# The log sum of the fourth opening block as two passes of an exact pair

## The chip, the cores and the metric

The kernel runs on one core of one Trainium2 chip. The core has five engines that work side by side and wait for each other by semaphores: TensorE (matrix products, PE in the profile; PEld is its loading of the stationary operand), VectorE (DVE), ScalarE (ACT), GpSimd (POOL) and SyncE (SP), which here issues the transfers. The metric is the device time of one execution in microseconds. Before the change the median of three runs is 516.35 us (516.2 to 517.95).

## The reference

A gated linear attention feeds a feed-forward layer with a squared ReLU. All of it is float32.

```python
# q, k, v, alpha: (4, 8, 768, 48); alpha between 0.8 and 1.0
for t in range(S):
    state = alpha[:, :, t, :, None] * state + einsum('bhd,bhe->bhde', k[:, :, t], v[:, :, t])
    y[:, :, t] = einsum('bhd,bhde->bhe', q[:, :, t], state)
x = y.transpose(0, 2, 1, 3).reshape(3072, 384)
h = maximum(x @ w_in, 0.0)            # w_in: (384, 2048)
return (h * h) @ w_out                # w_out: (2048, 384)
```

## The kernel before

The recurrence is done in chunks of 128 steps. A block is one chunk of one of the four sequences, with all eight heads side by side (128 x 384 values of each of q, k, v and alpha), so there are 24 blocks; block n is chunk n // 4 of sequence n % 4. Four blocks make a group of 512 tokens, and the feed-forward layer is done by groups, six in all. A block's attention goes in small steps, named by short words:

- `ln`: the logarithm of alpha, on ScalarE, in place.
- `cs`: the running sum of the logarithms over the 128 steps, a product with a triangle of ones on TensorE. In blocks from `AT['split']` on, a step `sp` ahead of it splits the logarithm into a pair: `hi`, the value rounded to TensorE's fast float32 type (fp32r), and `lo`, what is left of it, in the same type. The sum is then two fast passes, one over each part, into the same bank. In blocks below `AT['split']`, `cs` is one product in plain float32, which TensorE does as two passes at a lower rate.
- `eb`, `ei`: the exponential of that sum and of its negative, on ScalarE (tiles `b` and `inv`).
- `mq`, `mk`: q times `b` and k times `inv`, on VectorE.
- `qT`, `kT`: both turned round by TensorE; `qc`, `kc` copy the results (`qs`, `ks`) to where TensorE can read them.
- `sc`, `kv`, `am`, `us`, `st`, `lt`: the scores within a chunk, the sums for the state, the mask, and the state of the next chunk.
- `ya`, `yb`: the products that give y for two blocks; `ep` copies y into the feed-forward layer's input `x`, on ScalarE and VectorE.
- `ha`, `hb`: the first layer of the feed-forward for half a group.
- `load`, `weights`: transfers; `first`, `second`: the weights' conversion to float32, on ScalarE and VectorE.

The order of the work is the program's: each engine takes its instructions in the order in which the program writes them, and there is no scheduler that changes it. For the first blocks (the opening, about the first 35 us) that order is the string `AT['first']` in line 22, which is read word by word (line 1004): the word `ln3` calls `ln(3)`, the step of the fourth block. Everything behind the opening is woven from lists of due times (`weave`, line 1113). Transfers all go through SyncE's queue in `move` (line 108), which also holds one back until an earlier one has landed.

Lines that matter for the change: 261 (`ln`), 273 and 274 (`sp`: hi, lo), 283 (`cs` in one product), 286 and 287 (`cs` in two passes), 294 and 298 (`eb`, `ei`), 302 (`mq`, `mk`), 354 (`qT`, `kT`), 368 (the copies `qs`, `ks`), 393 (y), 621 (the copies x<-y), 942 (first layer in the first group). The blocks' tiles `b` and `hi` take turns in one pool of two buffers, and `inv` and `lo` in another.

Of the kernel before, what the change touches and what calls it, by code (L numbers as in the profile page):

```python
# [18 lines left out]


GB = 4
AT = {'sq': (12, 6, 5, 11), 'hi': (12, 13, 11, 10), 'ips': 0, 'evs2': 0.3, 'tc': 'AAAD', 'rest': 0, 'lg': 9, 'lag': 1, 'post2': 1, 'ty': 9, 'thrp': 3.5, 'cvo': 2.9, 'thr': 2.25, 'm48': 16, 'cvs': 3.6, 'cv1': 0.25, 'later': (0, 2, 0, 4, 1, 4, 2), 'evs': 0.35, 'lead': 4, 'post': 3, 'w_first': (48.95, 42.05, 53.75), 'wstep': 0.8, 'w_in_at': 1.25, 'w_in_by': 2.9, 'room1': 23, 'room': 24, 's0': 4, 'ahead': 6, 'late': 2, 'xs': 0.55, 'g0': ((3.25, 4, False, True, 32.0), (22.75, 6, True, True), (26.5, 8, True, False)), 'sc0': (2.95, 2.35, 2.35), 'g1': ((2.75, 8, False, 16.25), (15.5, 10, True), (31.75, 12, True)), 'g': ((2.075, 6, True), (13.75, 8, True)), 'g1x': 49.0, 'gx': 46.25, 'g0x': 55.25, 'k0': 3, 'h0': 12, 'k1': 5, 'h1': 6, 'h1by': 2, 'evs0': 0.3, 'tp': 'ADAD', 'tp1': 'AADA', 'split': 4, 'o0': (34, 46, 46), 'o1': (), 'o2': (16.75, 19.25, 30.75, 23.0, 38.0), 'str1': 10.0, 'ga': 9.5, 'gb': 12.25, 'cv0': -1.125, 'pre': '1a 0a 0q 0k 1k 1q', 'cp': ('q2a', 'k2b', 'k0a', 'k3a', 'k3b', 'k0b', 'q0b', 'q3b', 'q2b', 'q3a'), 'evd': ((0, 0, 0), (0, 0, 1), (0, 1, 2), (0, 1, 3), (2, 0, 3), (2, 1, 1), (2, 1, 2)), 'first': 'ln0 load1v cs0 ei0 eb0 zeros4 mk0 mq0 qT0 kT0 ln1 cs1 kc0 ei1 warm0 load0v eb1 mk1 qc0 weights0 lt1 sc0 load2a mq1 load2q kT1 kc1 qT1 load2k load3a qc1 load3k kv0 am0 first0 load3v sc1 ln2 kv1 load3q us0 am1 weights6 us1 cs2 ya0 ei2 second0 eb2 lt0 ln3 yb0 load2v mq2 qT2 mk2 load4a ep00 ep01 qc2 kT2 cs3 kc2 eb3 ei3 zeros1 sc2 ep02 mq3 mk3 kT3 ep03 weights2 first1 st0 ha0 second1 lt2 kv2 am2 qT3 load4k kc3 qc3 ha1 weights5 first2 sc3 kv3 am3 load4q us2 ha2 us3 ya2 yb2 weights3 ep20 ep21 ep22 load4v ep23 second2 first3 weights1 st1 weights4 ha3 lt3 hb0 st2 second3 hb2 hb3 hb1 st3'}


RUN = {0: 128, 32: 32, 64: 64, 96: 32}
# [3 lines left out]
def kernel(  # L29
# [78 lines left out]
    def move(us, out, in_):  # L108
        ins = nc.sync.dma_start(out=out, in_=in_).ins  # L109
        ahead = 0.0  # L110
        for before, took in reversed(under_way):
            if ahead >= AT["thrp" if us == 1.0 else "thr"]:
                tc.add_manual_dep(
# [16 lines left out]
    def load(n, xs="aqkv"):  # L130
        c, b = divmod(n, B)
        for x in xs:
            t = tile_of(x, n)
            if id(t) in owner:
                need(("free", *owner[id(t)]))
            owner[id(t)] = x, n
            given.add((x, n))
            move(
                1.1,
                out=t[:, :, 0:D] if x in "qk" else t.rearrange("a (h d) -> a h d", h=H),  # L140
                in_=srcs[x][b, :, c * C : (c + 1) * C, :].rearrange("h s d -> s h d"),
            )
# [57 lines left out]

    for word in AT["pre"].split():
        load(int(word[0]), word[1:])
# [52 lines left out]
    def work(name, bufs=1):  # L255
        return p2.tile([128, NP, C], FP32, tag=name, name=name, bufs=bufs)
# [7 lines left out]

    SPLIT = AT["split"]

    def sp(n):
# [4 lines left out]
        lo = p2.tile([128, H * D], FP32R, tag="inv", name="lo")  # L272
        (nc.scalar.copy if n in AT["hi"] else nc.vector.tensor_copy)(out=hi, in_=la)
        nc.vector.tensor_tensor(out=lo, in0=la, in1=hi.bitcast(FP32), op=ALU.subtract)
# [90 lines left out]
    def copied(x, n):  # L365
        t = blk[n][f"{x}s"] = work(f"{x}s", 2 if x == "k" else 4)
        copy = nc.vector.tensor_copy if f"{x}{n}" in AT["cp"] else nc.scalar.copy
        copy(out=t, in_=blk[n].pop(f"{x}T"))
# [64 lines left out]
    def state_sums(n):  # L433
        need(("v", n), ("kb", n))
        given.add(("free", "k", n))
        ps = two[n]
        m = D if n >= AT["m48"] else 64
        for p in range(NP):
# [805 lines left out]
```

## Time and profile before

| what | value |
| --- | --- |
| median of the runs | 516.35 us |
| lowest, highest of three runs | 516.2, 517.95 us |
| the profiled execution's own time | 516.38 us |
| its span, from the first to the last instruction | 514.6 us |
| TensorE busy | 504.5 us (98%) |
| VectorE busy | 357.7 us (70%) |
| ScalarE busy | 315.5 us (61%) |
| granted clock of TensorE, mean | 1.000 |

All times in the tables of a profile are microseconds from the start of the span. A line of a timeline gives the start, the length, the engine, the line of the kernel, the operation, what it writes and reads, its shape, and how often it stands there in a row; in brackets stands how long the engine had been idle before it and what it was waiting for. Consecutive instructions of one engine can overlap by a little, since they are pipelined. SPq, DVEq and the like are an engine's queue rather than its arithmetic. "issue" is time in which nothing that the profile shows was waited for.

### The profile page before, as it was taken

What the parts mean: (1) busy time and instruction counts of PE and PEld (TensorE: products, weight loads), DVE (VectorE), ACT (ScalarE), POOL (GpSimd) and SP (SyncE); (2) the same over time, 40 slices, a digit from 0 to 9 for tenths busy, and PEclk for the clock granted to TensorE, in tenths of its full rate; (3) what the DMA queues carried; (4) which work ended last, traced back from release to release, by engine and by line L of the source; (5) the groups of instructions that cost most, each with busy time, mean ns of one, the idle gap of its engine ahead of it and who ended that gap; (6) DMA issues with size and microseconds to landing.
All of it is one profiled execution on the core that took longest, in us unless ns stands there. A gap on an engine that the chain in (4) does not pass through costs nothing.

```text
span 514.6 us, 13039 instructions
## 1 busy us (share of the span) xinstructions
PE 504.5 (98%) x5354; PEld 421.1 (82%) x5354; DVE 357.7 (70%) x640; ACT 315.5 (61%) x657; POOL 5.3 (1%) x29
## 2 busy tenths in 40 slices
PE   7799999999999999999999999999999999999997
PEld 5675456689888689888899987799988899988996
DVE  3769799989887498585697377596465396263861
ACT  4789896466988674368672186783175782165620
POOL 4000000000000000000000000000000000000000
PEclk9999999999999999999999999999999999999999
DMA  9899867484869649986984787684673554798101
GB/s 182 201 264 236 271 180 190 107 235 187 274 195 256 164 101 272 333 228 183 227 233 134 262 235 200 173 247 131 231 253 125 182 143 142 251 373 292 61 1 62
DMA packets 139612, 103.12 MB, mean 200 GB/s; under 512 B 109841, under 2 KB 116001, under 8 KB 139553
## 3 DMA queue, kind: packets, MB, share of 16 engines
q1 hardware_dynamic: 139552, 102.30, 69.0%
q8 instruction: 42, 0.69, 0.5%
q14 instruction: 18, 0.14, 0.1%
HBM read 84.95 MB, written 17.33 MB: 199 GB/s over the span
## 4 chain that ended last, share of the span: by engine, by line
PE 94%; DMA 4%; SPq 1%; ACT 0%; DVE 0%; issue 0%; DVEq 0%; POOLq 0%
PE o L825 41%; PE h L731 33%; PE h L942 8%; PE y L393 4%; PE sckv L413 2%; PE T L581 2%; DMA k_in<-in_k_dram 2%; PE sckv L442 2%; DMA qk_lent<-in_q_dram 1%; DMA v_in<-in_v_dram 1%; PE cs L286 1%; PE cs L287 1%; SPq L109 1%; ACT x L621 0%; DVE x L621 0%
## 5 line engine op out<-in xcount | busy, mean ns | idle before, releaser
L731 PE MATMUL h<-xa,wb 128*128 128x512 f32 x240 | 68.9, 395 | 0.0
L731 PE MATMUL h<-xl,wl 128*128 128x512 f32 x240 | 67.7, 390 | 0.0
L731 PE MATMUL h<-xd,wd 128*128 128x512 f32 x240 | 67.2, 395 | 0.0
L748 ACT ACTIVATE h<-h 128x512 f32<-128x512 f32 x44 | 25.6, 581 | 59.0 <-PE h L731 59.0
L825 PE MATMUL o<-wb,ha 128*128 128x384 f32 x176 | 60.0, 341 | 0.0
L825 PE MATMUL o<-wl,hl 128*128 128x384 f32 x176 | 58.9, 335 | 0.0
L621 ACT COPY x<-y 48x256 f32<-48x256 f32 (+3 forms) x133 | 46.6, 366 | 18.7 <-PE y L393 15.8
L825 PE MATMUL o<-wd,hd 128*128 128x384 f32 x320 | 56.4, 334 | 0.0
L825 PEld LDWEIGHTS o<-wd,hd 128*128 128x128 f32 x320 | 55.6, 188 | 0.0
L653 DVE TENSOR_TENSOR hid<-h,hid 128x512 f32<-128x512 f32 x36 | 24.8, 689 | 43.4 <-PE h L731 43.2
L731 PEld LDWEIGHTS h<-xl,wl 128*128 128x128 f32 x240 | 45.1, 188 | 9.8
L731 PEld LDWEIGHTS h<-xa,wb 128*128 128x128 f32 x240 | 44.2, 188 | 9.8 <-ACT qs L591 0.8
L731 PEld LDWEIGHTS h<-xd,wd 128*128 128x128 f32 x240 | 44.2, 188 | 9.4
L825 PE MATMUL o<-wb,hx 128*128 128x384 f32 x144 | 48.2, 335 | 0.0
L825 PE MATMUL o<-wl,hx 128*128 128x384 f32 x144 | 48.1, 334 | 0.0
L942 PE MATMUL h<-x,w_in 128*128 128x512 f32 (+1 forms) x120 | 43.3, 512 | 0.2 <-DVE x L621 0.2
L825 PE MATMUL o<-w_out,hid 128*128 128x384 f32 x128 | 43.1, 490 | 0.0
L706 ACT ACTIVATE ha<-hid 128x512 fp32r<-128x512 f32 x44 | 27.0, 636 | 17.2 <-DVE hl L658 7.4
L825 PEld LDWEIGHTS o<-w_out,hid 128*128 128x128 f32 x128 | 23.9, 190 | 15.6 <-issue 0.5
L746 ACT ACTIVATE hid<-h 128x512 f32<-128x512 f32 x36 | 21.5, 597 | 24.3 <-PE h L731 24.3
L942 PEld LDWEIGHTS h<-x,w_in 128*128 128x128 f32 x120 | 22.1, 190 | 17.3 <-issue 14.8
L658 DVE SCALAR_TENSOR_TENSOR hl<-ha,hid 128x512 fp32r<-128x512 f32 x44 | 30.2, 686 | 6.1 <-ACT ha L706 6.1
(113 smaller groups left out, 867.1 us busy)
## 6 DMA issues: line engine op xcount, KB each, us to landing
wd<-do SPq DMA_DIRECT2D x37, 384.0 KB, 3.6
wl<-lo SPq DMA_DIRECT2D x35, 384.0 KB, 4.3
wl<-li SPq DMA_DIRECT2D x32, 384.0 KB, 2.9
wd<-di SPq DMA_DIRECT2D x32, 384.0 KB, 3.8
raw<-in_moe_w_out_dram SPq DMA_DIRECT2D x8, 767.5 KB
raw<-in_moe_w_in_dram SPq DMA_DIRECT2D x8, 767.2 KB
v_in<-in_v_dram SPq DMA_DIRECT2D x24, 192.0 KB, 3.7
out_dram<-osb SPq DMA_DIRECT2D x24, 192.0 KB, 1.8
```

What stands on the lines that cost most here:

```text
L393: ins = nc.tensor.matmul(out=ys[e][64 * half : 64 * half + D + G * e, m % 2, p // 2, t], lhsT=lhsT, rhs=rhs, start=(half, e) not in seen, ...
L413: nc.tensor.matmul(out=ps[e][HALF[h], 0, p, :], lhsT=ks[rows, p, HALF[h]], rhs=qs[rows, p, HALF[h]], start=True, stop=True, skip_group_che ...
L442: nc.tensor.matmul(out=ps[h][64 * e : 64 * e + m, 1, p, G:64], lhsT=tile_of("k", n)[HALF[h], 2 * p + e, 0:m], rhs=tiles["v"][n % NV][HALF[ ...
L621: copy(out=x[kk][to : to + m, t : t + 2], in_=blk[n]["y"][e][r : r + m, :, p // 2],)
L653: nc.vector.tensor_tensor(out=o, in0=x, in1=z, op=op)
L658: nc.vector.scalar_tensor_tensor(out=o, in0=x, scalar=c, in1=y, op0=ALU.mult, op1=op)
L706: nc.scalar.activation(out=a, in_=x, func=AF.Copy, scale=NEAR * E)
L731: nc.tensor.matmul(out=acc["h", j], lhsT=here[w, "i", p][:, kk, jj * 128 : (jj + 1) * 128], rhs=x_parts[x][:, kk], start=start and kk == 0 ...
L746: nc.scalar.activation(out=hid[j], in_=x, func=AF.Copy, scale=E)
L748: nc.scalar.activation(out=x, in_=x, func=AF.Copy, scale=1.0 + E)
L825: nc.tensor.matmul(out=acc[t][:, 0:DM], lhsT=lhs[:, t * C : (t + 1) * C], rhs=rhs, start=start, stop=stop, skip_group_check=True,)
L942: nc.tensor.matmul(out=ps, lhsT=w[:, kk, c0 : c0 + 128], rhs=xT[g][kk][:, cols], start=(kk == 0), stop=(kk == KM - 1),)
```

## The change

Block 3, the fourth and last block of the first group, gets its logarithm split too. `AT['split']` goes from 4 to 3, so that `sp(3)` and the two passes of `cs(3)` take the place of the one product, and the word `sp3` is put into the opening's order directly behind `ln3`, ahead of `yb0` and of the third block's `mq2` and `mk2`. Block 3 isn't listed in `AT['hi']`, so both instructions of the step go to VectorE.

```diff
 AT = {
...
-'split': 4,
+'split': 3,
...
-'first': '... us1 cs2 ya0 ei2 second0 eb2 lt0 ln3 yb0 load2v mq2 qT2 mk2 load4a ep00 ep01 qc2 kT2 cs3 kc2 eb3 ei3 zeros1 sc2 ep02 mq3 mk3 kT3 ep03 weights2 ...'
+'first': '... us1 cs2 ya0 ei2 second0 eb2 lt0 ln3 sp3 yb0 load2v mq2 qT2 mk2 load4a ep00 ep01 qc2 kT2 cs3 kc2 eb3 ei3 zeros1 sc2 ep02 mq3 mk3 kT3 ep03 weights2 ...'
...
 }
```

The step and the two forms of the sum are there already, for the later blocks:

```python
def sp(n):
    if n < SPLIT:
        return
    la = blk[n].pop("la")
    hi = p2.tile([128, H * D], FP32R, tag="b", name="hi")
    lo = p2.tile([128, H * D], FP32R, tag="inv", name="lo")
    (nc.scalar.copy if n in AT["hi"] else nc.vector.tensor_copy)(out=hi, in_=la)
    nc.vector.tensor_tensor(out=lo, in0=la, in1=hi.bitcast(FP32), op=ALU.subtract)
    blk[n]["parts"] = hi, lo

def cs(n):
    given.add(("free", "a", n))
    ps = blk[n]["cs"] = bank(n, "cs")
    out = ps.rearrange("a p t -> a (p t)")[:, 0 : H * D]
    if n < SPLIT:
        nc.tensor.matmul(out=out, lhsT=causal_r.bitcast(FP32), rhs=blk[n].pop("la"), start=True, stop=True)
        return
    hi, lo = blk[n].pop("parts")
    nc.tensor.matmul(out=out, lhsT=causal_r, rhs=hi, start=True, stop=False)
    nc.tensor.matmul(out=out, lhsT=causal_r, rhs=lo, start=False, stop=True)
```

More of the change, by code (lines that the diff above doesn't have):

```diff
@@ L21 @@
 GB = 4
-AT = {'sq': (12, 6, 5, 11), 'hi': (12, 13, 11, 10), 'ips': 0, 'evs2': 0.3, 'tc': 'AAAD', 'rest': 0, 'lg': 9, 'lag': 1, 'post2': 1, 'ty': 9, 'thrp': 3.5, 'cvo': 2.9, 'thr': 2.25, 'm48': 16, 'cvs': 3.6, 'cv1': 0.25, 'later': (0, 2, 0, 4, 1, 4, 2), 'evs': 0.35, 'lead': 4, 'post': 3, 'w_first': (48.95, 42.05, 53.75), 'wstep': 0.8, 'w_in_at': 1.25, 'w_in_by': 2.9, 'room1': 23, 'room': 24, 's0': 4, 'ahead': 6, 'late': 2, 'xs': 0.55, 'g0': ((3.25, 4, False, True, 32.0), (22.75, 6, True, True), (26.5, 8, True, False)), 'sc0': (2.95, 2.35, 2.35), 'g1': ((2.75, 8, False, 16.25), (15.5, 10, True), (31.75, 12, True)), 'g': ((2.075, 6, True), (13.75, 8, True)), 'g1x': 49.0, 'gx': 46.25, 'g0x': 55.25, 'k0': 3, 'h0': 12, 'k1': 5, 'h1': 6, 'h1by': 2, 'evs0': 0.3, 'tp': 'ADAD', 'tp1': 'AADA', 'split': 4, 'o0': (34, 46, 46), 'o1': (), 'o2': (16.75, 19.25, 30.75, 23.0, 38.0), 'str1': 10.0, 'ga': 9.5, 'gb': 12.25, 'cv0': -1.125, 'pre': '1a 0a 0q 0k 1k 1q', 'cp': ('q2a', 'k2b', 'k0a', 'k3a', 'k3b', 'k0b', 'q0b', 'q3b', 'q2b', 'q3a'), 'evd': ((0, 0, 0), (0, 0, 1), (0, 1, 2), (0, 1, 3), (2, 0, 3), (2, 1, 1), (2, 1, 2)), 'first': 'ln0 load1v cs0 ei0 eb0 zeros4 mk0 mq0 qT0 kT0 ln1 cs1 kc0 ei1 warm0 load0v eb1 mk1 qc0 weights0 lt1 sc0 load2a mq1 load2q kT1 kc1 qT1 load2k load3a qc1 load3k kv0 am0 first0 load3v sc1 ln2 kv1 load3q us0 am1 weights6 us1 cs2 ya0 ei2 second0 eb2 lt0 ln3 yb0 load2v mq2 qT2 mk2 load4a ep00 ep01 qc2 kT2 cs3 kc2 eb3 ei3 zeros1 sc2 ep02 mq3 mk3 kT3 ep03 weights2 first1 st0 ha0 second1 lt2 kv2 am2 qT3 load4k kc3 qc3 ha1 weights5 first2 sc3 kv3 am3 load4q us2 ha2 us3 ya2 yb2 weights3 ep20 ep21 ep22 load4v ep23 second2 first3 weights1 st1 weights4 ha3 lt3 hb0 st2 second3 hb2 hb3 hb1 st3'}
@@ new lines @@
+AT = {'sq': (12, 6, 5, 11), 'hi': (12, 13, 11, 10), 'ips': 0, 'evs2': 0.3, 'tc': 'AAAD', 'rest': 0, 'lg': 9, 'lag': 1, 'post2': 1, 'ty': 9, 'thrp': 3.5, 'cvo': 2.9, 'thr': 2.25, 'm48': 16, 'cvs': 3.6, 'cv1': 0.25, 'later': (0, 2, 0, 4, 1, 4, 2), 'evs': 0.35, 'lead': 4, 'post': 3, 'w_first': (48.95, 42.05, 53.75), 'wstep': 0.8, 'w_in_at': 1.25, 'w_in_by': 2.9, 'room1': 23, 'room': 24, 's0': 4, 'ahead': 6, 'late': 2, 'xs': 0.55, 'g0': ((3.25, 4, False, True, 32.0), (22.75, 6, True, True), (26.5, 8, True, False)), 'sc0': (2.95, 2.35, 2.35), 'g1': ((2.75, 8, False, 16.25), (15.5, 10, True), (31.75, 12, True)), 'g': ((2.075, 6, True), (13.75, 8, True)), 'g1x': 49.0, 'gx': 46.25, 'g0x': 55.25, 'k0': 3, 'h0': 12, 'k1': 5, 'h1': 6, 'h1by': 2, 'evs0': 0.3, 'tp': 'ADAD', 'tp1': 'AADA', 'split': 3, 'o0': (34, 46, 46), 'o1': (), 'o2': (16.75, 19.25, 30.75, 23.0, 38.0), 'str1': 10.0, 'ga': 9.5, 'gb': 12.25, 'cv0': -1.125, 'pre': '1a 0a 0q 0k 1k 1q', 'cp': ('q2a', 'k2b', 'k0a', 'k3a', 'k3b', 'k0b', 'q0b', 'q3b', 'q2b', 'q3a'), 'evd': ((0, 0, 0), (0, 0, 1), (0, 1, 2), (0, 1, 3), (2, 0, 3), (2, 1, 1), (2, 1, 2)), 'first': 'ln0 load1v cs0 ei0 eb0 zeros4 mk0 mq0 qT0 kT0 ln1 cs1 kc0 ei1 warm0 load0v eb1 mk1 qc0 weights0 lt1 sc0 load2a mq1 load2q kT1 kc1 qT1 load2k load3a qc1 load3k kv0 am0 first0 load3v sc1 ln2 kv1 load3q us0 am1 weights6 us1 cs2 ya0 ei2 second0 eb2 lt0 ln3 sp3 yb0 load2v mq2 qT2 mk2 load4a ep00 ep01 qc2 kT2 cs3 kc2 eb3 ei3 zeros1 sc2 ep02 mq3 mk3 kT3 ep03 weights2 first1 st0 ha0 second1 lt2 kv2 am2 qT3 load4k kc3 qc3 ha1 weights5 first2 sc3 kv3 am3 load4q us2 ha2 us3 ya2 yb2 weights3 ep20 ep21 ep22 load4v ep23 second2 first3 weights1 st1 weights4 ha3 lt3 hb0 st2 second3 hb2 hb3 hb1 st3'}
```

## The prediction, made before the result was known

> **What bounds the kernel now.** I read the page first, then the busy time by stretches, the chain of waits in order of time, and last the timelines of VectorE, ScalarE and TensorE around the place of the change. The page:
>
> ```profile
> span 514.6 us, 13039 instructions
> PE 504.5 (98%) x5354; PEld 421.1 (82%) x5354; DVE 357.7 (70%) x640; ACT 315.5 (61%) x657; POOL 5.3 (1%) x29
> ```
>
> TensorE (PE) is busy for all but 10.1 us of the span, so the question is only where those idle microseconds lie. The stretches say it (columns: PE, PEld, DVE, ACT, POOL busy with their counts, granted clock, DMA share, GB/s):
>
> ```profile
> 20.00:30.00 10.00, 8.58 (x177) 6.97 (x177) 7.79 (x17) 8.61 (x20) 0.00 (x0) 1.00 0.89 240
> 30.00:40.00 10.00, 9.66 (x147) 7.57 (x144) 6.76 (x16) 8.84 (x20) 0.00 (x0) 1.00 0.88 264
> 40.00:50.00 10.00, 10.00 (x29) 5.18 (x28) 9.52 (x20) 9.05 (x18) 0.00 (x0) 1.00 1.03 223
> ```
>
> From 40 us on PE has no idle time (50 to 300 us: 250.00 busy of 250; 300 to 400: 99.72) until the last 5 us. Whatever makes PE late before 40 us is therefore carried to the end; nothing behind it can take it up. Before 40 us PE waits, and the chain of waits tells for what (start, length, what):
>
> ```profile
> 17.33 5.48 DMA qk_lent<-in_q_dram
> ...
> 22.90 0.06 DVE qk_lent L302
> ...
> 23.38 0.56 DVE qk_lent L302
> ...
> 24.08 0.63 PE kT L354 x4
> ...
> 33.50 0.36 ACT x L621
> ...
> 36.76 12.31 PE h L942 x38
> ```
>
> The fourth block's q arrives at 22.81; VectorE scales q (step mq3, 22.90) and k (mk3, 23.38); PE turns k (kT3) at 24.08 and is dense from there, but for the hand-over of the second pair's result at 33.5 to 36.8, which follows from PE's own y at 33.47. The last thing that isn't already PE's own order is thus VectorE's arrival at mq3. VectorE's queue before it (start, length, engine, line, operation):
>
> ```profile
> 18.43 0.96 DVE L199 TENSOR_TENSOR w_in<-w_in,power 128x768 f32<-128x768 f32 x1
> 19.30 0.55 DVE L302 TENSOR_TENSOR qk_lent<-qk_lent,b 128x384 f32<-128x384 f32 x1
> 19.77 0.55 DVE L302 TENSOR_TENSOR k_in<-k_in,inv 128x384 f32<-128x384 f32 x1
> 20.33 2.22 DVE L621 COPY x<-y 48x256 f32<-48x256 f32 x5
> 22.90 0.56 DVE L302 TENSOR_TENSOR qk_lent<-qk_lent,b 128x384 f32<-128x384 f32 x1 [0.35 <-DMA qk_lent<-in_q_dram]
> ```
>
> It runs without a gap from before 18.43 to 22.55 and then waits 0.35 us for q. That 0.35 us is the only room here. The other two engines:
>
> ```profile
> 19.39 0.52 ACT L261 ACTIVATE a_lent<-a_lent 128x384 f32<-128x384 f32 x1
> 20.00 0.63 PE L354 MATMUL qT<-ident,qk_lent 128*128 128x128 f32 x4 [0.39 <-DVE qk_lent L302]
> 24.08 0.63 PE L354 MATMUL kT<-ident,qk_lent 128*128 128x128 f32 x4 [1.30 <-DVE qk_lent L302]
> ```
>
> The first is ln3, the logarithm that the new step reads; it ends at 19.91. PE already stands waiting for VectorE at both transposes.
>
> **The change part by part.** On VectorE two instructions (sp3: hi, then lo) go in ahead of mq2. ScalarE, POOL and SP keep their instructions and order, so no DMA is added or moved in its queue. On PE one fp32 product becomes two fp32r passes in the same place. What the new instructions cost is shown by the same step of a later block:
>
> ```profile
> 47.45 0.35 DVE L273 CAST hi<-a_in 128x384 fp32r<-128x384 f32 x1
> 47.84 0.56 DVE L274 TENSOR_TENSOR lo<-a_in,hi 128x384 fp32r<-128x384 f32 x1
> 48.32 0.68 DVE L653 TENSOR_TENSOR hid<-r 128x512 f32<-128x512 f32 x1
> ```
>
> 1. *The wait for the logarithm.* VectorE would be free for its next instruction at 19.30, but hi reads ln3's result, done at 19.91; ScalarE to VectorE takes 0.04 (power ends at 26.67, its reader starts at 26.71). hi starts at 19.95: 0.65 us of new standing still. Its other wait, for PE's lastT of the first block, is over at 18.99. Queued behind: mq2, mk2, five copies x<-y, mq3, mk3.
>
> 2. *The two instructions.* hi to lo 0.39, lo to the next 0.48 (starts above): mq2 starts at 19.95 + 0.87 = 20.82 instead of 19.30, 1.52 later. mk2 follows at 21.29, the copies at 21.85 (0.56 behind mk2, as now), ending at 24.07. The copies wait for ScalarE copies that end by 21.07, no longer felt.
>
> 3. *What 0.35 us takes back.* mq3 no longer waits for q (landed at 22.81). It starts behind the last copy, 0.03 after its end as the next instruction behind such a copy does at 24.38 to 24.41: 24.10 instead of 22.90. mk3 starts at 24.58, ends at 25.13, and kT3 comes 0.15 behind it: 25.28 instead of 24.08. This is 1.52 - 0.35 + 0.03 = **1.20 us**.
>
> 4. *The side branches, costed at nothing.* qT2, kT2 move by 1.52, to 21.52 and 21.99, so qs2 on ScalarE starts at 22.19, ks2 at 22.67, eb3 at 23.14, ei3 at 23.53, ending at 24.02. The cover is VectorE's own lateness: mq3 needs eb3 (23.63) by 24.10, and mk3 needs ei3 (24.02) by 24.58. That leaves 0.47 and 0.56. Were that gone, each 0.1 of ScalarE would go straight into kT3. eb3 and ei3 get new waits for VectorE, as hi and lo take turns with b and inv in two buffers each: for lo (20.90) and mk2 (21.84), both long past. PE's own pass of the sum, sc2 and kT3 are queued behind qT2; sc2 then starts at 23.3, clear of kT3.
>
> 5. *The two passes.* Before: 0.81 us for the fp32 sum (20.93). After: two passes at 0.53 (0.19 apart plus 0.34, back to back) up to 0.91 (48.51 to 49.42, a pass behind another shape). From 22.45 that ends at 22.98 to 23.36, against eb3's slot at 23.14: at worst eb3 is 0.26 later, inside the 0.47. PE's gain of up to 0.28 us lies ahead of a wait of PE and is worth nothing. I take 0 for either end.
>
> 6. *Downstream.* PE from 24.08 to 33.47 is dense; then ScalarE's copies (33.50) and VectorE's (34.28, 35.83), then dense to the end: all of it starts from kT3 or from y, so +1.20 goes on unchanged. ScalarE's wait for a weight transfer at 30.70 (0.9 us) shrinks, but PE doesn't stand behind it: ScalarE, free at 29.83 now and so at 31.03 then, does 2.2 us of work there (two power steps, r, hid) and is free again at about 33.3, before y at 34.67.
>
> Sum: the profiled execution took 516.38 us (span 514.6 and 1.8 around it); plus 1.20 is 517.58. It stands 0.03 above the median of the runs, 516.35, so I forecast **517.55 us**, +0.23%. The bounds of its own terms: +0.9 (hand-overs some 0.05 shorter at each of six places) to +1.55 (the 0.35 not got back), 517.25 to 517.9.
>
> **The rivals.** *A colder TensorE (slower by over 0.5%).* Early in the span products run at half speed:
>
> ```profile
> 5.14 1.62 PE L283 MATMUL cs<-a_in,causal_r 128*128 128x384 f32 x2 [1.12 <-ACT a_in L261]
> 9.63 0.81 PE L283 MATMUL cs<-a_in,causal_r 128*128 128x384 f32 x2
> ```
>
> The same two passes take 1.62 us at 5.14 and 0.81 at 9.63, while the granted clock reads 1.00 in both stretches, so only durations tell it. Later gaps don't bring it back: after PE idles 1.30 us up to 24.08, h runs at 0.22 a pass (six in 1.46, the last 0.38 long), half the 0.42 and more of the first products. From sc2's end (22.77) to h (24.54) PE does only transposes, 1.77 us. After the change y ends at 19.61 and PE idles until 21.52, 1.9 us, and its first product that is no transpose is the log sum at 22.45, 2.8 us after y. No row shows so long a gap. Were it enough, PE would have to warm up once more: in the opening that held 4.4 us of busy PE (1.10 to 4.03 and 5.14 to 6.6) at half speed, 2.2 us lost, so 516.35 + 1.20 + 2.2 = 519.75. It decides if the limit lies between 1.8 and 2.8 us. The Trainium skill ("TensorE: Matmul & The Clock Gate", Part 1 and Part 4) says the clock halves after an idle window of about 3.4 us, and that transposes do not count as busy in the same way; the second speaks against this change, the first still spares it, and no run here shows either limit. Chance 0.08.
>
> *Hidden behind q (not slower).* If the transfer of the fourth q usually lands later than here, mq3 waits for it in both kernels: landing at 24.0 or later would leave nothing of the 1.20, 516.35. For it: the transfer took 5.48 us of a crowded queue. Against: the profiled execution, with q at 22.81, is within 0.03 us of the median. Chance 0.08 for +0.3 or less.
>
> *The split isn't where it says.* Had hi gone to ScalarE (0.50 us in later rows), ln3's followers there would slip. Block 3 isn't among those the table sends to ScalarE: excluded.
>
> **How the numbers follow.** About 0.5%, 2.6 us, is what a measurement of this kernel can tell from no change: 513.77 to 518.93. The forecast case has 0.78, the cold clock 0.08, hidden 0.08, and 0.06 is left for what I don't see (one of three runs stands 1.6 us above the others). The cold clock and 0.01 of the rest lie above 518.93: slower 0.09. No mechanism gains 2.6 us where PE's waits for VectorE are 0.39 and 1.30: faster 0.01. Same 0.90. The range reaches half-way to the two rivals, 516.7 to 518.8, and leaves out some 0.17.
>
> **What would show it.** Right: hi starts within 0.1 of ln3's end, mq2 1.5 late, no DMA wait ahead of mq3, kT3 at 25.2 to 25.4, h x38 at 37.9 to 38.0, and the rest shifted as it stands. Wrong: mq3 still waits for q (hidden); passes of h around 25 to 30 us at over 0.3 us each (cold); eb3 or ei3 as what releases mq3 or mk3 (step 4); or PE taking up time behind 40 us.

## The result and the profile after

The changed kernel took 518.36 us (median of 19 runs, 517.44 to 521.93), the kernel before 516.79 us beside it (19 runs, 515.97 to 519.18): a ratio of 1.0041, 95% interval 1.0029 to 1.0054. It is slower, by 1.57 us between the medians. The ratio is not the quotient of the two medians, which is 1.0030; it lies near that of the means, 518.94 and 516.94 us, which are 2.00 us apart. The forecast was 517.55 us and +1.20.

The lateness that was forecast is there, and something more. The profiled execution of the changed kernel took 521.24 us (span 519.4), at the upper end of its runs, with a mean granted clock of 0.989. Its page, the totals and the row of the granted clock in 40 slices of 13 us:

```profile
PE 508.8 (98%) x5354; PEld 424.8 (82%) x5354; DVE 358.5 (69%) x642; ACT 315.6 (61%) x657; POOL 5.3 (1%) x29
PEclk9879999999999999999999999999999999999999
```

PE executes as many instructions as before, and is busy 4.3 us longer with them; the second and third slice of the clock are short. The windows of 2 us (length, then busy time and count of PE, PEld, DVE, ACT and POOL, then the granted clock, DMA share, GB/s) show where:

```profile
20.00:22.00 2.00, 0.27 (x3) 0.30 (x4) 1.80 (x5) 1.23 (x4) 0.00 (x0) 1.00 0.92 273
22.00:24.00 2.00, 2.00 (x25) 1.72 (x27) 1.89 (x6) 1.61 (x4) 0.00 (x0) 0.76 1.10 268
24.00:26.00 2.00, 1.62 (x35) 1.43 (x28) 1.89 (x5) 1.35 (x5) 0.00 (x0) 0.50 0.78 178
32.00:34.00 2.00, 2.00 (x21) 1.39 (x22) 0.00 (x0) 0.42 (x2) 0.00 (x0) 0.68 0.96 278
34.00:36.00 2.00, 2.00 (x69) 1.84 (x62) 1.04 (x4) 1.97 (x4) 0.00 (x0) 1.00 1.09 292
```

The granted clock falls to 0.50 at 23.06 us and is back at 33.30, by the trace's records of the clock; the 0.76 and the 0.68 of the rows say the same to 0.02 us. Shortly before, from 19.84 to 21.73, PE had stood still. The timeline of DVE in the changed kernel:

```profile
18.65 0.96 DVE L199 TENSOR_TENSOR w_in<-w_in,power 128x768 f32<-128x768 f32 x1
20.16 0.36 DVE L273 CAST hi<-a_lent 128x384 fp32r<-128x384 f32 x1 [0.55 <-ACT a_lent L261]
20.55 0.56 DVE L274 TENSOR_TENSOR lo<-a_lent,hi 128x384 fp32r<-128x384 f32 x1
21.03 0.55 DVE L302 TENSOR_TENSOR qk_lent<-qk_lent,b 128x384 f32<-128x384 f32 x1
21.97 2.21 DVE L621 COPY x<-y 48x256 f32<-48x256 f32 x5
24.11 0.53 DVE L302 TENSOR_TENSOR qk_lent<-qk_lent,b 128x384 f32<-128x384 f32 x1
24.58 0.54 DVE L302 TENSOR_TENSOR qk_lent<-qk_lent,inv 128x384 f32<-128x384 f32 x1
```

It waits 0.55 us for the logarithm, makes hi and lo, and only then comes to mq2 (21.03), the copies and mq3, which no longer waits for a transfer. PE in the same execution:

```profile
19.14 0.69 PE L393 MATMUL y<-am,v_in 64*48 64x64 f32 x32
21.73 0.63 PE L354 MATMUL qT<-ident,qk_lent 128*128 128x128 f32 x4 [1.89 <-DVE qk_lent L302]
22.58 0.42 PE L286 MATMUL cs<-hi,causal_r 128*128 128x384 f32 x1
22.84 0.34 PE L287 MATMUL cs<-lo,causal_r 128*128 128x384 f32 x1
23.54 1.25 PE L413 MATMUL sckv<-qs,ks 48*64 48x64 f32 x32
25.17 1.12 PE L354 MATMUL kT<-ident,qk_lent 128*128 128x128 f32 x4 [0.38 <-DVE qk_lent L302]
26.08 2.77 PE L942 MATMUL h<-x,w_in 128*128 128x256 f32 x6
```

Behind y it is idle for 1.89 us instead of 0.39. From sc2 on everything takes nearly double: six passes of h 2.77 us, where the kernel before has 1.46.

That is one kind of execution. The kernel before and the changed one were run again later, and that profile of the changed kernel (517.92 us, span 516.1, clock 0.999) has the same wait and no fall:

```profile
19.34 0.69 PE L393 MATMUL y<-am,v_in 64*48 64x64 f32 x32
21.93 0.63 PE L354 MATMUL qT<-ident,qk_lent 128*128 128x128 f32 x4 [1.89 <-DVE qk_lent L302]
25.37 0.66 PE L354 MATMUL kT<-ident,qk_lent 128*128 128x128 f32 x4 [0.96 <-DVE qk_lent L302]
25.86 1.46 PE L942 MATMUL h<-x,w_in 128*128 128x256 f32 x6
```

The granted clock sorts the 19 runs: four at 0.989 to 0.990 (mean 521.61 us), eight at 0.995 to 0.997 (518.21), seven at 0.999 to 1.000 (518.26). A fall of 3.41 us anywhere lowers the mean clock of a run by 0.003, one of 10.24 us by 0.010; below, a run with a mean clock of 0.997 or less is counted as one with a fall. Of 90 runs of the kernel before beside the experiments, seven are at 0.992 to 0.993, none is lower, and none lies between that and 0.998. Six of the seven are among the 29 runs of the last comparison.

### The profile page after: what moved, and what is told of

Read it like the earlier page. It is cut to its first block, busy times and chain, and to the rows that moved or that the text cites. A ratio compares the mean times of both kernels' runs of the same rounds, so it can differ in the third digit from the quotient of the medians.

```text
span 519.4 us, 13042 instructions
## 1 busy us (share of the span) xinstructions
PE 508.8 (98%) x5354; PEld 424.8 (82%) x5354; DVE 358.5 (69%) x642; ACT 315.6 (61%) x657; POOL 5.3 (1%) x29
## 4 chain that ended last, share of the span: by engine, by line
PE 96%; ACT 1%; DVE 1%; DMA 1%; issue 0%; SPq 0%; POOLq 0%; DVEq 0%
PE o L825 41%; PE h L731 32%; PE h L942 8%; PE y L393 5%; PE sckv L413 2%; PE T L581 2%; PE sckv L442 2%; PE cs L286 1%; PE cs L287 1%; DMA a_in<-in_alpha_dram 1%; PE cs L283 1%; DVE x L621 1%; ACT x L621 0%; PE kT L354 0%; PE qT L354 0%; ACT power L179 0%
## 5 line engine op out<-in xcount | busy, mean ns | idle before, releaser
L621 ACT COPY x<-y 48x256 f32<-48x256 f32 (+3 forms) x133 | 46.6, 366 | 19.6 <-PE y L393 17.0
L942 PE MATMUL h<-x,w_in 128*128 128x512 f32 (+1 forms) x120 | 45.6, 534 | 0.2 <-DVE x L621 0.2
L942 PEld LDWEIGHTS h<-x,w_in 128*128 128x128 f32 x120 | 23.7, 203 | 17.8 <-issue 14.8
```

The source lines that it names most:

```text
L621: copy(out=x[kk][to : to + m, t : t + 2], in_=blk[n]["y"][e][r : r + m, :, p // 2],)
L942: nc.tensor.matmul(out=ps, lhsT=w[:, kk, c0 : c0 + 128], rhs=xT[g][kk][:, cols], start=(kk == 0), stop=(kk == KM - 1),)
```

## The experiments

The theory was the prediction's: the two instructions make VectorE late, and nothing else matters. Its rivals were that PE's long wait lets its clock fall, and that the pair or its two passes cost something by themselves. All times below are medians. The runs were made in three groups of four, each on another chip and with the kernel before beside it: the first four experiments below (kernel before 516.26 us); the first run of the warm products without added instructions, the pair made twice, the same work elsewhere and the earlier kT3 (516.78 us); the second run of those warm products, the pair without lateness, and both kernels again (517.14 us).

**Warm products in the gap.** Six products of zeros, read by nobody, behind y.

```diff
-lt0 ln3 sp3 yb0 load2v mq2
+lt0 ln3 sp3 yb0 zeros6 load2v mq2
```

> The changed kernel with six products of zeros (128x128 each) put on TensorE behind the first pair's y, where it now idles 1.9 us waiting for VectorE's mq2; they take about 1.4 us and delay nothing. Theory A (the change costs 1.2 us by VectorE's lateness in every execution, and in some executions TensorE's clock falls to half because of that idle stretch): the lowest times stay near 517.4 us, kT3 stays about 1.1 us late, no execution shows a mean clock of 0.99, the median falls from 518.4 to about 517.6 us and nothing lies above 519. Theory B (the excess over 1.2 us comes from the new work itself, its two passes and its tiles, and the clock falls whatever stands in the gap): median 518.4 us as before, one execution in five near 521.6 us with a clock of 0.99.

Measured: 518.65 us (518.03 to 521.31), ratio 1.0050 (1.0032 to 1.0068). PE in the profiled execution (520.8 us), the opening and the place where it lost time:

```profile
21.75 0.62 PE L354 MATMUL qT<-ident,qk_lent 128*128 128x128 f32 x4 [0.36 <-DVE qk_lent L302]
25.19 0.66 PE L354 MATMUL kT<-ident,qk_lent 128*128 128x128 f32 x4 [0.96 <-DVE qk_lent L302]
25.68 1.46 PE L942 MATMUL h<-x,w_in 128*128 128x256 f32 x6
...
230.71 0.68 PE L393 MATMUL y<-am,v_in 64*48 64x64 f32 x27
233.38 0.33 PE L393 MATMUL y<-am,v_in 64*48 64x64 f32 x4 [1.98 <-issue]
234.44 1.34 PE L731 MATMUL h<-xl,wl 128*128 128x512 f32 x3
```

In this execution the opening kept its clock and the lateness stayed, as it should if the gap makes the clock fall. But the kernel was not quicker, against the forecast of 517.6 us and nothing above 519. Eight runs without a fall took 518.0 to 519.0 us, and four with a clock of 0.995 to 0.997 took 520.2 to 521.3. The profiled execution is one of these four: at 231.40 us PE stood for 1.98 us with nothing that the profile shows to wait for, and the clock fell there, from 234.6 for 3.41 us. A 16 KB transfer on the instruction queue (q8) began 0.4 us before that standstill. The added products put twelve more products ahead of all later ones of PE, so this run could not tell the gap from the code, and the fill was made again without adding an instruction.

**The pair made, and not used.** hi and lo are made at the same place, but the sum is the one plain product of before.

```diff
-        la = blk[n].pop("la")
+        la = blk[n]["la"] if n == 3 else blk[n].pop("la")
...
-        if n < SPLIT:
+        if n <= SPLIT:
```

> The changed kernel in which VectorE still makes hi and lo, but the log sum of the fourth block is the one float32 product of the logarithm, as in the kernel before; the two parts are read by nobody. Theory A: as the changed kernel, median 518.2 to 518.6 us, lowest 517.4 us, and one execution in five or so at 521 us or more with a mean clock of 0.99. Theory B: at most 517.6 us and no execution at 0.99.

Measured: 518.64 us (517.62 to 520.01), ratio 1.0043 (1.0028 to 1.0057), as slow as the change. Its profile shows the fall as well, sooner, from 21.0 to 24.4 us, so that already the transposes are slow:

```profile
21.16 1.09 PE L354 MATMUL qT<-ident,qk_lent 128*128 128x128 f32 x4 [1.89 <-DVE qk_lent L302]
22.90 1.49 PE L283 MATMUL cs<-a_lent,causal_r 128*128 128x384 f32 x2
26.12 0.63 PE L354 MATMUL kT<-ident,qk_lent 128*128 128x128 f32 x4 [0.79 <-DVE qk_lent L302]
```

The two passes on PE are no part of the loss that is seen here; VectorE's two instructions alone cost as much as the whole change. Eight of the 12 runs have a fall, one of them at 0.992; none is near 521 us, as the expectation had it for one in five. The four without a fall have a median of 518.50 us, 2.2 above the kernel before, so the falls are not the larger part of the loss here.

**The logarithm earlier.** ln3 and the pair ahead of lt0, which takes away most of VectorE's wait for ln3.

```diff
-second0 eb2 lt0 ln3 sp3 yb0
+second0 eb2 ln3 sp3 lt0 yb0
```

> The changed kernel with the fourth block's logarithm put ahead of the copies of the first block's lastT on ScalarE, which stood idle there: hi no longer waits for it, starts some 0.65 us earlier, and mq2 is 0.87 instead of 1.52 us late. Theory A: kT3 and all behind it 0.5 to 0.6 us later than in the kernel before instead of 1.2, TensorE's gap before qT2 about 1.25 us; lowest 516.5 to 516.7 us, median 516.9 to 517.3 us, no execution at a clock of 0.99. Theory B: lowest also 0.6 us lower, but one execution in five stays some 4 us longer.

Measured: 517.39 us (516.21 to 519.52), ratio 1.0015 (1.0000 to 1.0031); one of 12 runs below a clock of 0.998.

**The pair later.** hi and lo behind mk2, so that qT2 is not late and the lateness goes into mq3 alone.

```diff
-lt0 ln3 sp3 yb0 load2v mq2 qT2 mk2 load4a
+lt0 ln3 yb0 load2v mq2 qT2 mk2 sp3 load4a
```

> The changed kernel with hi and lo behind mk2 instead of ahead of mq2 on VectorE. mq2, mk2, qT2 and kT2 are then as in the kernel before; the copies x<-y and with them mq3 are 0.87 - 0.35 + 0.03 = 0.55 us late. Theory A: lowest 516.5 to 516.7 us; TensorE's gap before qT2 is again 0.4 us and that before kT3 grows from 1.3 to about 1.85 us with transposes at its end, so if a fully idle stretch of 1.9 us were enough for the clock to fall some executions would show 0.99, and if the transposes in front of it count as idle too (2.8 us in the changed kernel, 2.3 us here) fewer; median 516.9 to 517.6 us. Theory B: one execution in five at 0.99 as in the changed kernel.

Measured: 517.49 us (516.57 to 519.43), ratio 1.0019 (1.0004 to 1.0035); two of 12 runs below 0.998. The gap has moved from qT2 to kT3:

```profile
20.07 0.63 PE L354 MATMUL qT<-ident,qk_lent 128*128 128x128 f32 x4 [0.39 <-DVE qk_lent L302]
24.47 0.63 PE L354 MATMUL kT<-ident,qk_lent 128*128 128x128 f32 x4 [1.63 <-DVE qk_lent L302]
24.93 1.46 PE L942 MATMUL h<-x,w_in 128*128 128x256 f32 x6
```

Both versions keep the pair and lose half of what the two before them on the same chip lose (1.1 and 1.2 us instead of 2.4 between the medians), and neither has a fall in its profile.

**Warm products without added instructions.** The four products of zeros of 128 columns at the start (`zeros4`) become one of 512 columns, and three of 256 columns (`zeros3`) go into the gap; PE's count stays at 5354.

```diff
-lt0 ln3 sp3 yb0 load2v mq2
+lt0 ln3 sp3 yb0 zeros3 load2v mq2
...
-        for _ in range(n):
+        w = NP if n == 3 else 2 * NP if n == 4 else NP // 2
+        for _ in range(3 if n == 3 else 1):
...
-                out=ps[:, 0 : NP // 2, :], lhsT=s_t[3].rearrange("a p d -> a (p d)")[:, 0:128],
+                out=ps[:, 0 : w, :], lhsT=s_t[3].rearrange("a p d -> a (p d)")[:, 0:128],
...
```

> The changed kernel with TensorE's 1.9 us gap filled again by products of zeros, but with as many products in the program as the changed kernel has: three of 256 columns in the gap (about 1.3 us), paid for by making the four of 128 columns in the opening one of 512. The first fill added twelve products, and its profile showed, beside a steady clock in the opening, a standstill of TensorE of 1.98 us at 231.4 us that nothing releases, beginning 0.4 us behind a 16 KB instruction transfer. Theory A (lateness, and a clock that falls after the gap): no execution at 0.99 and none near 0.996 by the opening. If the standstill came with the shifted instruction stream, the median is 517.2 to 517.9 us, lowest 516.8 to 517.2; if it came with the lateness itself, the median stays at 518.4 to 518.9 us as in the first fill.

Measured: ratio 1.0021 (1.0003 to 1.0039), timed runs between 517.18 and 520.26 us, one of eight (520.26) at a clock of 0.992. The profiled execution took 2251 us as a whole, and nothing is read from it; so the kernel was run once more, with others beside it:

> The fill of TensorE's gap at an unchanged number of products once more, since its profiled execution was disturbed as a whole (2251 us). Theory A: median 0.9 to 1.4 us above the kernel before (the lateness, and no fall of the clock in the opening), the clock 0.998 or more in nearly all executions, kT3 0.8 to 1.1 us late against the end of y, no standstill of 2 us at 231 us. If the clock falls whatever stands in the gap: as the changed kernel, 1.6 us and more, with executions near 521 us.

Measured then: 517.75 us (517.09 to 518.43, 12 runs, none below a clock of 0.999), ratio 1.0001 (0.9983 to 1.0019). The kernel before beside it has six long runs with a fall, which raise what the ratio compares with; its 23 others have a median of 516.86, so the filled kernel is 0.9 us above those. The changed kernel beside it has 517.91 us with seven of 12 runs below 0.998:

```profile
19.07 1.56 PE L382 MATMUL zeros<-s 128*128 128x256 f32 x6
21.03 0.63 PE L354 MATMUL qT<-ident,qk_lent 128*128 128x128 f32 x4 [0.40 <-DVE qk_lent L302]
24.47 0.66 PE L354 MATMUL kT<-ident,qk_lent 128*128 128x128 f32 x4 [0.96 <-DVE qk_lent L302]
```

With the gap filled, this comparison has no fall, and no long run (521.27 in the one, 518.43 in the other). The median moves by 0.16 us only: the falls make long runs, not the usual ones.

**The pair made twice.** As the unused pair, but both instructions twice: double the lateness, and a longer gap.

```diff
-        (nc.scalar.copy if n in AT["hi"] else nc.vector.tensor_copy)(out=hi, in_=la)
-        nc.vector.tensor_tensor(out=lo, in0=la, in1=hi.bitcast(FP32), op=ALU.subtract)
+        for _ in range(2 if n == 3 else 1):
+            (nc.scalar.copy if n in AT["hi"] else nc.vector.tensor_copy)(out=hi, in_=la); nc.vector.tensor_tensor(out=lo, in0=la, in1=hi.bitcast(FP32), op=ALU.subtract)
```

> The kernel with the unused pair, in which VectorE makes hi and lo twice over: the delay of mq2 grows by another 0.87 us to 2.39, TensorE's gap before qT2 to about 2.75 us (3.65 us from y to the first product that is no transpose), kT3 by 0.87. Theory A: the clock falls in most executions: more than half at a mean clock of 0.997 or less in a kernel whose undisturbed time is about 519.4 us, median 519.8 to 522 us. If falls of the clock have nothing to do with the gap: as the unused pair made once plus 0.87, 519.5 us, with as many falls as there.

Measured: 520.36 us (519.50 to 522.30), ratio 1.0074 (1.0059 to 1.0088). All six runs are at a clock of 0.997 or less.

```profile
23.21 1.09 PE L354 MATMUL qT<-ident,qk_lent 128*128 128x128 f32 x4 [2.88 <-DVE qk_lent L302]
28.16 0.63 PE L354 MATMUL kT<-ident,qk_lent 128*128 128x128 f32 x4 [0.79 <-DVE qk_lent L302]
```

**The same work where VectorE has time.** Two instructions of the same kind and size, on data that nobody needs, in the kernel before, behind st0.

```diff
-first1 st0 ha0 second1
+first1 st0 idle0 ha0 second1
...
+    def idle(_):
+        t, m = cv_pool.tile([128, 2, DM], FP32R, tag="upper", name="spare"), am_t[1].rearrange("a e p t -> a (e p t)")[:, 0:DM]
+        nc.vector.tensor_copy(out=t[:, 0], in_=m)
+        nc.vector.tensor_tensor(out=t[:, 1], in0=m, in1=t[:, 0].bitcast(FP32), op=ALU.subtract)
```

> The kernel before, unchanged, with two more VectorE instructions of the same kinds and sizes as hi and lo (on other data, read by nobody) where VectorE idles 1.5 us, behind the first state (25.2 us). Nothing waits for them. If the time beyond the lateness comes with the lateness (transfers and TensorE's instruction fetches meet differently): 516.0 to 516.6 us, as the kernel before. If it comes with two more instructions in VectorE's stream: 516.8 to 517.3 us.

Measured: 516.92 us (515.98 to 519.22), ratio 1.0005 (0.9992 to 1.0018): VectorE's 0.9 us cost nothing where it isn't waited for. Its profiled execution (518.9 us) happens to be one with a fall, at another place: the opening ran ahead there, PE waited longer for the third block's logarithm, and the clock was at 0.50 from 18.0 to 21.4 us.

```profile
17.64 1.38 PE L283 MATMUL cs<-a_lent,causal_r 128*128 128x384 f32 x2 [2.60 <-ACT a_lent L261]
18.95 1.13 PE L393 MATMUL y<-qs,us 48*48 48x64 f32 x32
```

So a fall comes without the change too, where PE happens to stand for so long; two of these 12 runs have one.

**An earlier kT3.** The kernel before, with the fourth block's k ahead of its q, to see what PE gains if kT3 is early.

```diff
-cs3 kc2 eb3 ei3 zeros1 sc2 ep02 mq3 mk3 kT3
+cs3 kc2 ei3 eb3 zeros1 sc2 ep02 mk3 mq3 kT3
```

> The kernel before with the fourth block's ei and mk ahead of its eb and mq, on ScalarE and VectorE: the turning of k on TensorE, which waits for mk alone, then doesn't wait for the arrival of q. mk3 starts at about 22.55 instead of 23.38, kT3 at 23.2 to 23.4 instead of 24.08. If what the chain of waits ends with sets the end, 0.6 to 0.85 us less than the kernel before: median 515.4 to 515.8 us. If any shift of the opening against the transfers costs some 0.8 us of fetches met badly, as the excess of the late kernels suggests: 516.0 to 516.6 us.

Measured: 516.31 us (515.62 to 518.72), ratio 1.0003 (0.9991 to 1.0014), no change clear of the noise, though kT3 starts 1.08 us sooner than in the profile of before. The 0.6 to 0.85 us that this was to gain are not there.

```profile
21.92 0.69 PE L413 MATMUL sckv<-qs,ks 48*64 48x64 f32 x32 [0.46 <-ACT ks L368]
23.00 0.63 PE L354 MATMUL kT<-ident,qk_lent 128*128 128x128 f32 x4 [0.39 <-DVE qk_lent L302]
```

**The pair, and no lateness.** The changed kernel with ln3 and the pair earlier and the fourth block's k first, both from above.

```diff
-eb2 lt0 ln3 sp3 yb0 ... kc2 eb3 ei3 zeros1 sc2 ep02 mq3 mk3 kT3
+eb2 ln3 sp3 lt0 yb0 ... kc2 ei3 eb3 zeros1 sc2 ep02 mk3 mq3 kT3
```

> The changed kernel with the lateness taken out: the fourth block's logarithm ahead of the first block's lastT copies (hi 0.65 us earlier), and its ei and mk ahead of eb and mq, so that kT3 waits for mk3 in mq3's place. The pair, its two passes and both VectorE instructions stay. kT3 should come 3.8 to 4.0 us behind the end of y (19.61 in the kernel before, kT3 24.08: 4.47 us there, about 5.35 in the changed kernel), so 0.2 us or more earlier than in the kernel before. Theory A: 516.2 to 517.0 us beside a kernel before of 516.3 to 516.8, no worse than it by more than 0.6 us. If the pair itself costs time beside the lateness: over 517.3 us.

Measured: 517.14 us (516.24 to 518.00), the kernel before beside it 517.14 us, ratio 1.0004 (0.9989 to 1.0020). kT3 is not late, and the loss is gone within that interval with the pair still there (0.3 us are left against the 516.86 of the runs of the kernel before without a fall). What becomes of an early kT3 is seen further on in the same timeline of PE:

```profile
23.71 0.66 PE L354 MATMUL kT<-ident,qk_lent 128*128 128x128 f32 x4 [0.49 <-DVE qk_lent L302]
24.20 1.50 PE L942 MATMUL h<-x,w_in 128*128 128x256 f32 x6
...
29.06 0.69 PE L413 MATMUL sckv<-qs,ks 48*64 48x64 f32 x32 [0.40 <-ACT qs L368]
```

Here PE stands for 0.40 us at the next scores, for ScalarE's copy of q; in the kernel before there is no wait at that place (28.89). In the earlier kT3 above it is 0.56 us at 28.43. A later kT3 is paid for in full; of an earlier one 0.4 to 0.6 us is taken back 5 us on. No version was quicker than the kernel before by more than the noise.

**Both kernels again.** The changed kernel, and one profiled execution of the kernel before.

> The changed kernel once more, for a second profile and more times beside the others. Theory A (0.9 us of lateness, a clock that falls after the gap in part of the executions, and instruction fetches that meet the transfers worse when the opening is shifted): 1.3 to 2.2 us above the kernel before in the median, some executions at a clock of 0.99; in the profile kT3 0.8 to 1.2 us behind the end of the first pair's y compared with the kernel before (or more, if the clock fell there), and standstills of TensorE behind 40 us of 0.2 to 1.5 us in sum. If the excess were chance between chips, the median lies 0.9 us above the kernel before.

> The kernel before once more, for a second profile of it: standstills of TensorE behind 40 us that nothing releases should again sum to about 0.3 us (0.28 in its first profile, 0.33 with the two idle instructions), against 0.2 to 2.0 us (mean 0.9) in the seven profiles of shifted openings. If it has 0.8 us or more, the standstills have nothing to do with the shift.

Measured: the changed kernel 517.91 us (517.67 to 521.27), ratio 1.0020 (1.0001 to 1.0040), so half the first result's difference, and nearer to the 0.9 us that was expected for chance between chips than to the 1.3 to 2.2 of the theory; the kernel before, one execution, 517.07 us. Beside these, six of 29 runs of the kernel before had a fall (519.06 to 519.85); the remaining 23 have a median of 516.86, the ten runs of the changed kernel above 0.99 one of 517.88: +1.0 us. VectorE and PE in the kernel before, this time:

```profile
21.03 2.22 DVE L621 COPY x<-y 48x256 f32<-48x256 f32 x5
23.18 0.53 DVE L302 TENSOR_TENSOR qk_lent<-qk_lent,b 128x384 f32<-128x384 f32 x1
23.65 0.54 DVE L302 TENSOR_TENSOR qk_lent<-qk_lent,inv 128x384 f32<-128x384 f32 x1
19.62 0.69 PE L393 MATMUL y<-am,v_in 64*48 64x64 f32 x32
24.33 0.63 PE L354 MATMUL kT<-ident,qk_lent 128*128 128x128 f32 x4 [0.86 <-DVE qk_lent L302]
```

Here mq3 does not wait for q at all; in the profile the prediction was made from it waited 0.35 us. Behind 40 us PE stands still for 0.41 us in this profile, which lies between the 0.3 and the 0.8 that the expectation set apart, so it does not decide whether the change lengthens such standstills.

**Where PE's time went, in all profiles but the disturbed one.** PE's lateness against the first profile of before, in microseconds, split by starts of the same instructions: up to the last y of the second block ("opening"), from there to kT3, and from there to PE's last product.

| kernel | opening | y to kT3 | behind kT3 | end |
| --- | --- | --- | --- | --- |
| changed | +0.23 | +0.86 | +3.75 (fall, 10.24 us) | +4.84 |
| changed, again | +0.42 | +0.87 | +0.24 | +1.53 |
| six products in the gap | +0.24 | +0.87 | +3.29 (standstill, fall) | +4.40 |
| same count, gap filled | -0.47 | +0.86 | +1.12 | +1.51 |
| pair unused | -0.34 | +2.38 (fall) | +0.24 | +2.28 |
| pair twice | +0.72 | +3.36 (fall) | +0.32 | +4.40 |
| logarithm earlier | +0.76 | +0.22 | +0.69 | +1.67 |
| pair later | +0.07 | +0.32 | +1.20 | +1.59 |
| pair, not late | -0.14 | -0.23 | +1.08 | +0.71 |
| before, k first | -0.15 | -0.93 | +0.97 | -0.11 |
| before, work added behind st0 | +2.60 (fall) | -0.43 | +0.34 | +2.51 |
| before, again | +0.71 | -0.46 | +0.41 | +0.66 |

## Why the prediction was right or wrong

*Step 1, the wait for ln3: right.* Counted from the end of y, which comes 0.22 later in this execution, hi starts at 19.94 (forecast 19.95), 0.03 behind ln3's end.

*Step 2, the two instructions: right.* mq2 starts at 20.81 on the same count (20.82), qT2 is 1.5 us late, PE idle for 1.89 us (1.9).

*Step 3, mk3 and kT3: the mechanism is right, the size was off.* The wait for q is gone, as forecast. The copies, mq3 and the hand-over to kT3 came about 0.1 sooner each than was reckoned, and kT3 is 0.87 later against y instead of 1.20, in the first profile of the change as in its second and in both with the gap filled. And the 0.35 that was taken back was that of one execution: in the kernel before's second profile there is no such wait, y to kT3 is 0.46 shorter (0.43 in the kernel before with work added behind st0), and against that one the change costs 0.87 + 0.46 = 1.33. By these two profiles of before the term of the sum is 0.9 to 1.3 us; the larger goes with the later opening (+0.71 at y).

*Step 4, ScalarE's branches, and step 5, the two passes, both at nothing: right.* mq3 and mk3 wait for nothing of ScalarE, and the unused pair is as slow as the used one.

*Step 6, that the lateness goes on unchanged: right without a fall, and one-sided.* ScalarE's wait for the weights vanished, as reckoned. An early kT3 is not carried on.

*The rival of the colder TensorE: this is the step that failed.* The term was left out of the sum and made a case that happens or doesn't, with a chance of 0.08 and a price of 2.2 us. The prediction's own sign of it showed in the first profile: passes of h at 0.46 us (six in 2.77). It happens in a part of the executions: falls in 12 of the 19 runs, then in 7 of 12 and, with the unused pair, 8 of 12; in 6 of 6 with the pair twice; in 1 and 2 of 12 with a gap of 1.26 or 1.63 us; in one of 20 with the gap filled at the same count (both times together), and in four of 12 with the six added products, whose profile has it far from the gap. Mostly it is one window of 3.41 us, at a time when PE is waiting anyway, and in the changed kernel's means nothing is seen of it (518.21 against 518.26, and 517.86 against 518.08; with the unused pair 518.88 against 518.51). In 4 of 19 and 2 of 12 runs it is longer and costs 2.8 to 3.4 us (521.61 less 518.23; 520.73 less 517.97). That raises the mean by 4/19 of 3.4, or 0.7 us, in the first comparison, and leaves the median where it is. Of the 2.00 us between the means, 0.7 is thus the long falls and 0.9 to 1.3 the lateness of kT3; the kernel before beside it has one run above 519 us.

Two limits of this. Falls of one window and those at 0.988 to 0.990 are not seen in the 90 runs of the kernel before, so they go with the gap (with work added behind st0 one of 12 runs has a fall of one window, behind a gap of 2.60 us, and the version without lateness has a run at 0.997); but the kernel before has falls of its own, at 0.992 to 0.993, and in the last comparison these were as frequent (six of 29, at a cost of 2.6 us by the means) as the changed kernel's long ones (two of 12). There the falls explain nothing of the difference. And the price of 2.2 us came from a stretch of half speed that was read too short (last section).

*The rival that hides it behind q: excluded* as a whole (no wait for q is left), though it was on the right track: the kernel before does hide a late opening behind that wait.

*What the usual runs have beyond that.* The median difference was 1.57 in the first comparison and +1.0 without the long falls in the last; kT3's 0.9 to 1.3 covers the second and most of the first. It does not cover the first four experiments: without a fall, the unused pair (518.50) and the six products (518.43) stand 2.2 us above the kernel before beside them (516.25), and the two versions whose kT3 is only 0.2 to 0.3 us late stand 1.0 and 1.2 above it. Of these, 0.3 to 1.3 us, by which profile of before is taken, are without an explanation. In the profiles the rest lies behind kT3, where the first profile of before is the least of all that have no fall: the kernel before itself came out 0.41 later there the second time, and 0.44 us of the forecast's distance from the result (518.36 less 517.55) is that the kernel before took 516.79 us beside it, not 516.35. The larger of these differences behind kT3 are mostly standstills of PE that the profile puts down to nothing, near 231, 310 and 38 us, of 0.2 to 2.0 us. That the change makes them longer was not shown.

## What to carry to other kernels

An instruction put into an engine's strict order costs what it delays, not what it does: the same 0.9 us was free behind st0, and ahead of mq2 it made kT3 0.9 to 1.3 us late and the kernel by that or more. When a change lengthens a wait of TensorE, the chance of a colder clock is to be reckoned as a share of executions with a price of its own, which shows in the mean and the highest time before it shows in the median. And a wait that takes lateness back in one profile is to be checked against a second one before it is put into a sum.

## What the runs showed of the hardware that was not expected

*The clock falls by windows of a fixed grid.* In the records of the granted clock every stretch between two changes is a whole number of 3.413 us: 13.65 (4), 3.41 (1), 10.24 (3), 17.07 (5), 225.28 (66), 505.17 us (148). So the stretch behind which the clock falls is known, and PE's idle time in it can be added up from the starts and lengths of its products (the profile models their ends, so the last digits are not sure):

| profile | window, us | PE idle in it, us | clock in the next |
| --- | --- | --- | --- |
| pair later | 22.8 to 26.2 | 1.63 | 1.00 |
| before | 22.6 to 26.1 | 1.30 | 1.00 |
| changed, again | 20.2 to 23.6 | 1.74 | 1.00 |
| pair, not late, at the kernel's end | 510.0 to 513.4 | 1.85 | 1.00 |
| pair later, at the kernel's end | 510.9 to 514.3 | 1.87 | 1.00 |
| pair unused | 17.6 to 21.0 | 1.77 | 0.50 |
| changed | 19.6 to 23.1 | 1.89 | 0.50 |
| six products, far on | 231.2 to 234.6 | 1.98 | 0.50 |
| before, work added behind st0 | 14.5 to 18.0 | 2.60 | 0.50 |
| pair twice | 19.7 to 23.1 | 2.75 | 0.50 |

In the opening the limit lies between 1.74 and 1.77 us, near half a window. Idle time alone does not set it: at the kernel's end 1.85 and 1.87 us were not enough. There products of 128x384 filled the rest of the window, and in the window with 1.77 small products of y did; whether that is the reason was not tested. The grid does not start with the kernel, so by the limit in the opening a gap of 1.89 us has at least 1.77 in one window in (3.41 - 1.89 + 0.24) / 3.41, about half of all executions (an estimate from this table); 27 of 43 were counted. A gap of 1.3 us can't reach it alone.

The Trainium skill ("TensorE: Matmul & The Clock Gate", Part 1) has this grid: a free-running window of 3413 ns, which the records here confirm to the digit. It says that the clock halves after an idle window of about 3.4 us, and its closing section warns of gaps above about 3 us; here 1.77 to 1.98 us were enough, and the measurement decides. Why the fall lasted one window in some executions and three in others, with PE busy all through the second, no run settled.

*The record of the clock begins with its first rise.* That is at 8.99 us in the profile of before and at 3.97 in that of the unused pair. The same eight products of zeros, first line before, second line unused pair:

```profile
6.56 1.91 PE L381 MATMUL zeros<-s 128*128 128x128 f32 x8
5.80 1.05 PE L381 MATMUL zeros<-s 128*128 128x128 f32 x8
```

So the 1.00 that the windows show ahead of that time is no reading, and the opening of before ran at half speed up to 8.99 us, not up to 6.6 as the prediction had it. By these times that was 6.8 us of busy PE (1.10 to 4.02 and 5.14 to 8.99), and half of it, 3.4 us, is lost. That is an estimate in place of the 2.2; the long falls, of 10.24 us in the profile that shows one, cost 2.8 to 3.4 us.

*Long standstills far from the change.* PE stood still for 1.98 us at 231.40 with nothing to wait for, and for 0.2 to 0.9 us near 231 and 310 us in other profiles, those of the kernel before included. Transfers of 16 KB on the instruction queue lie near some of them (one began at 231.0 there; in the profile of before it began at 228.7, and PE ran on at that place). Near 310 us, 12 of the 13 profiles besides the disturbed one have a standstill of 0.17 to 0.78 us, and each begins 1.6 to 2.3 us behind the start of such a transfer (in the profile of before 306.89 and 309.11). That PE waits there for its own code is a guess that no run tested.
